# One load stream for the expert weights, and the float64 conversion spread over all experts, in a fused scan, mixture-of-experts and feed-forward kernel

## The chip, the cores and the metric

The kernel runs on one core of a Trainium2 chip. The metric is the time of one execution on the device in microseconds (us); 1192.2 us is the median of three runs before the change. The engines are named as the profile names them: PE is the matrix engine (PEld its weight loads), DVE the vector engine, ACT the scalar engine, POOL the GpSimd engine, and SP the engine that issues most of the DMA transfers. Each engine works through its own instructions strictly in order.

## The reference, cut to what matters

Three stages follow each other. The first is a recurrent scan over 768 positions for 32 (batch, head) pairs; the change does not touch it. Its output, 3072 rows of 320 values, goes through eight experts, one per row, and then through a dense pair of layers whose weights are given as float64:

```python
    logits = x @ w_gate
    e_idx = np.argmax(logits, axis=1)
    ...
    gate_w = probs[np.arange(N), e_idx]
    eom = 1.0 / (1.0 + np.exp(-(x @ w_output_gate)))
    for e in range(E):
        mask = e_idx == e
        h = np.maximum(x[mask] @ w1[e], 0.0)
        ye = h @ w2[e]
        out[mask] = gate_w[mask, None] * eom[mask, e, None] * ye
...
    h = np.maximum(x @ w_in, 0.0)
    return (h * h @ w_out).astype(np.float32)
```

## The kernel before, in words

The scan fills the first 560 us. It leaves the rows sorted by expert in a DRAM tile `xsD`, with the logits of each row beside it. Then come the experts, one after the other, and then the dense pair. All of it is written with a hand schedule: instructions stand on each engine in the order in which the Python code emits them.

**Weights in two parts.** Each weight is split into a high and a low float32r part. A piece of up to 732 columns is loaded from DRAM into one of four `raws` buffers (L909, on SP), ACT copies it rounded to the high part (L922), and POOL subtracts to get the low part (L923). An expert has eight such pieces. They go to one of two `ring` buffers, so the next expert's weights are split while this expert runs.

**An expert on PE.** The first layer has eight steps f of eight matmuls each (L1185, writing a PSUM tile `ph`, of which there are three). After each step ACT takes the high part of the hidden values (L1253) and DVE the low part (L1254); only then is that `ph` free again. In the last three steps PE also transposes the next expert's rows (L1226), which ACT and DVE split (L1175 to L1179). The second layer is 64 matmuls (L1356). Pieces of the next expert's weights are taken in steps f below 6 and early in the second layer.

**Gate factors.** `gates` computes, from the logits in `xg`, the token number and the squared factor of each row, in ten short instructions (eight on DVE: L987 to L999). It is emitted step by step within the first layer, between the L1254 instructions. The result `gt` goes to the DRAM tile `gtD` in two writes, one right behind the other (L1342).

**The float64 weights.** `widths` turns pairs of 32-bit words into float32. One step is: load `q` (L1141), one ACT instruction (L1151), four DVE instructions (L1152 to L1155), one POOL add (L1156), one more DVE instruction (L1167). Sixteen steps convert the first matrix `wi` beside the second layers of the experts, mostly three per expert, and the result goes to DRAM (`wiD`) and comes back as pieces. Sixteen steps of 320 columns convert `wo`, beside the last expert and the first steps of the dense pair; `split_o` splits each result at once (L1199 on ACT, L1200 on POOL).

**The dense pair.** 96 steps of `stage1` (eight matmuls L1185; then ACT L1404, DVE L1405, ACT L1407, DVE L1408) and, two steps behind, `stage2` (twelve matmuls L1188 to L1190). Before the first step the factors are read back into `GT` (L1383) and DVE copies the token numbers (L1384).

Of the kernel before, what the change touches and what calls it, by code (L numbers as in the profile page):

```python
# [7 lines left out]
F32 = mybir.dt.float32  # L8
# [23 lines left out]
NP = 104  # partitions of the (head of pair at 0 / 64, feature) layout  # L32
# [38 lines left out]
def layout(r, k, v, w, a, b, moe_w_gate, moe_w_output_gate, moe_w1, moe_w2, moe2_w_in, moe2_w_out):  # L71
# [41 lines left out]
ORDER = [  # stage, chunk relative to the iteration, argument  # L113
# [38 lines left out]
TAIL = [  # the last two iterations: stage, chunk relative to the last one, argument  # L152
# [73 lines left out]
HEAD = [  # the stages before the first regular iteration: stage, chunk, argument  # L226
# [70 lines left out]
EARLY = [2, 3, 5, 0]  # the first chunks for which DVE does a share of GpSimd's work  # L297


def attention(ctx, tc, nc, A, K, R, nch=NCH, order=ORDER, head=HEAD, tail=TAIL):  # L300
# [20 lines left out]
    def early(shape):  # L321
        """part of the arena: the buffers here are done with some chunks before the end"""
# [74 lines left out]
    # ---- loads  # L397
# [33 lines left out]
    # ---- decays: W (before a token) and C (after it), scaled a, b, k  # L431
# [20 lines left out]
    def A_rec2(c):  # L452
        # third-order step: 1 / C = y (t^2 - 3 t + 3), t = C y
# [27 lines left out]
    # ---- a.b and a.k of all pairs of tokens of a chunk  # L481
# [56 lines left out]
    # ---- inverse of the unit triangular system: 16 x 16 blocks, then the pair  # L538
# [65 lines left out]
    # ---- state  # L604
# [82 lines left out]
    # ---- outputs  # L687
# [72 lines left out]
    # ---- routing  # L760
# [49 lines left out]
def program(tc, A, out, nch=NCH, order=ORDER):  # L810
    nc = tc.nc
    V, G, S_, P = nc.vector, nc.gpsimd, nc.scalar, nc.tensor
    with ExitStack() as top:
# [6 lines left out]
        wiD = dp.tile([128, 3 * F2], F32, name="wiD")  # L820
        cst = cp.tile([128, C_TRI], F32, name="cst")
# [23 lines left out]
        # ---- routing of 128 tokens  # L845
# [28 lines left out]
        def beyond():  # L874
            """whether there are rows beyond CAP, or decays out of range, or too few of the rows that are read ahead"""
# [22 lines left out]
        W1E = [732 * i for i in range(7)] + [5120, 5632]  # pieces of an expert's weights, the last 64 columns of the second ones apart  # L898
        W2I = [768 * i for i in range(9)]

        def pieces(slot, src, at, slots=4):
            """weights as the sum of two float32r parts, piece by piece"""
# [11 lines left out]
            for i in range(len(at) - 1):  # L914
                rw = ahead.pop(i)
                if at[i + 1] == 5632:  # high and low parts side by side
                    rw = rw.rearrange("p (f x)->p f x", x=64)
                    both = ring[slot][:, 5120:6144].bitcast(F32R).rearrange("p (f x)->p f x", x=128)
                    hi, lo = both[:, :, 0:64], both[:, :, 64:128]
                else:  # L920
# [551 lines left out]
```

## Time and profile before

| | |
|---|---|
| median of three runs | 1192.2 us (1192.02 to 1195.96) |
| span of the profiled execution | 1201.3 us |
| instructions in the profile | 31764 |
| PE busy | 1038.2 us, 86% of the span |
| DVE busy | 829.3 us, 69% |
| ACT busy | 652.6 us, 54% |
| POOL busy | 476.9 us, 40% |
| DMA, mean over the span | 96 GB/s |

No time of the profiled execution is recorded besides its span, which is 0.8% above the median of the other runs. Busy shares are averages over three stages with different limits, so the reader should look at stages: the scan ends at about 560 us, the first matmul of the experts stands at 560.5 us, and the dense pair begins at 830.4 us. PE is busy for 86% of the span, but its busy time also counts matmuls that ran at the lower of its two clock levels.

### The profile page before, as it was taken

What the parts mean: (1) busy time and instruction counts of PE and PEld (TensorE: products, weight loads), DVE (VectorE), ACT (ScalarE), POOL (GpSimd) and SP (SyncE); (2) the same over time, 40 slices, a digit from 0 to 9 for tenths busy, and PEclk for the clock granted to TensorE, in tenths of its full rate; (3) what the DMA queues carried; (4) which work ended last, traced back from release to release, by engine and by line L of the source; (5) the groups of instructions that cost most, each with busy time, mean ns of one, the idle gap of its engine ahead of it and who ended that gap; (6) DMA issues with size and microseconds to landing.
All of it is one profiled execution on the core that took longest, in us unless ns stands there. A gap on an engine that the chain in (4) does not pass through costs nothing.

```text
span 1201.3 us, 31764 instructions
## 1 busy us (share of the span) xinstructions
PE 1038.2 (86%) x13114; PEld 911.5 (76%) x13114; DVE 829.3 (69%) x1827; ACT 652.6 (54%) x1407; POOL 476.9 (40%) x465
## 2 busy tenths in 40 slices
PE   2688888888897778887988889998989999999997
PEld 2577777777786666767877778886879998998986
DVE  6999998989989999653675566536993434344442
ACT  6587786776686776672444434334443343443432
POOL 6556464554554645341455455435541010101011
PEclk9977785869576886787989899999999999999999
DMA  5843333333332332243576667535330000000000
GB/s 139 265 124 83 87 93 86 98 83 92 86 92 72 104 86 70 82 122 125 133 200 168 179 188 187 146 115 131 104 97 23 27 23 27 23 1 23 2 21 22
DMA packets 56236, 114.99 MB, mean 96 GB/s; under 512 B 14608, under 2 KB 30096, under 8 KB 54160
## 3 DMA queue, kind: packets, MB, share of 16 engines
q1 hardware_dynamic: 50656, 100.47, 30.9%
q0 software_dynamic: 2688, 8.88, 1.9%
q10 hardware_dynamic: 2736, 3.49, 0.9%
q8 instruction: 106, 1.74, 0.6%
q14 instruction: 50, 0.41, 0.1%
HBM read 89.39 MB, written 23.43 MB: 94 GB/s over the span
## 4 chain that ended last, share of the span: by engine, by line
PE 31%; DVE 12%; DMA 6%; ACT 2%; issue 1%; SPq 1%; POOL 0%; POOLq 0%; ACTq 0%; DVEq 0%
PE ph L1185 17%; PE po L1189 4%; PE po L1190 4%; PE po L1188 4%; DMA raws<-in_we_dram 2%; PE py L1356 2%; DMA q<-in_wi_dram 2%; DVE c L1153 1%; DVE hl L1408 1%; DVE q L1405 1%; DVE c L1167 1%; DVE gm L996 1%; DVE gt L997 1%; DVE gt L999 1%; DVE c L1154 1%
## 5 line engine op out<-in xcount | busy, mean ns | idle before, releaser
L1185 PE MATMUL ph<-x,ring 128*128 128x512 f32 (+2 forms) x1344 | 319.7, 387 | 27.2 <-DVE hw L1254 27.2
L1185 PEld LDWEIGHTS ph<-x,ring 128*128 128x128 f32 x1344 | 249.5, 197 | 63.0 <-DVE hw L1254 30.0
L923 POOL TENSOR_TENSOR ring<-raws,ring 128x732 fp32r<-128x732 f32 (+2 forms) x72 | 124.1, 1744 | 137.2 <-ACT ring L922 108.3
L1405 DVE TENSOR_TENSOR q<-r 128x512 f32<-128x512 f32 x96 | 73.0, 761 | 106.8 <-ACT r L1404 106.8
L1423 POOL DMA_INDIRECT out_dram<-o,TID x24 | 28.2, 1175 | 269.6 <-ACT o L1421 226.7
L1189 PE MATMUL po<-ring,hl 128*128 128x320 f32 x368 | 115.6, 314 | 7.3 <-DVE hl L1408 7.3
L1188 PE MATMUL po<-ring,hh 128*128 128x320 f32 x368 | 114.6, 311 | 2.8 <-ACT hh L1407 2.8
L474 POOL TENSOR_TENSOR arena<-arena 40x1024 f32<-40x1024 f32 x43 | 108.5, 2523 | 20.2 <-ACT arena L456 16.0
L1404 ACT ACTIVATE r<-ph 128x512 f32<-128x512 f32 x96 | 57.1, 595 | 108.6 <-PE ph L1185 108.6
L1190 PE MATMUL po<-ring,hh 128*128 128x320 f32 x368 | 114.2, 310 | 0.0
L1408 DVE TENSOR_TENSOR hl<-q,hh 128x512 fp32r<-128x512 f32 x92 | 72.5, 788 | 54.8 <-ACT hh L1407 54.8
L1407 ACT ACTIVATE hh<-q 128x512 fp32r<-128x512 f32 x92 | 58.2, 633 | 88.0 <-DVE q L1405 88.0
L1356 PE MATMUL py<-hw,ring 128*128 128x448 f32 x512 | 105.4, 365 | 0.0
L1356 PEld LDWEIGHTS py<-hw,ring 128*128 128x128 f32 x512 | 95.5, 188 | 7.6
L1254 DVE SCALAR_TENSOR_TENSOR hw<-ph,hw 128x448 fp32r<-128x448 f32 (+2 forms) x72 | 39.7, 567 | 88.2 <-ACT hw L1253 88.1
L1189 PEld LDWEIGHTS po<-ring,hl 128*128 128x128 f32 x368 | 69.6, 189 | 14.9 <-DVE hl L1408 11.1
L1188 PEld LDWEIGHTS po<-ring,hh 128*128 128x128 f32 x368 | 69.8, 190 | 7.5 <-ACT hh L1407 3.2
L450 POOL TENSOR_TENSOR arena<-Cx,arena 104x512 f32<-104x512 f32 x22 | 26.3, 1197 | 123.6 <-ACT xs L862 115.7
L1190 PEld LDWEIGHTS po<-ring,hh 128*128 128x128 f32 x368 | 69.7, 189 | 0.0
L922 ACT ACTIVATE ring<-raws 128x732 fp32r<-128x732 f32 (+2 forms) x72 | 56.9, 792 | 22.8 <-DMA raws<-in_we_dram 20.5
L1253 ACT ACTIVATE hw<-ph 128x448 fp32r<-128x448 f32 (+2 forms) x72 | 35.8, 498 | 57.8 <-PE ph L1185 57.6
L439 DVE TENSOR_TENSOR_SCAN Cx<-arena 104x528 f32<-104x528 f32 x24 | 61.0, 2540 | 7.0 <-DMA arena<-in_xE_dram 6.3
(215 smaller groups left out, 2257.7 us busy)
## 6 DMA issues: line engine op xcount, KB each, us to landing
raws<-in_we_dram SPq DMA_DIRECT2D x48, 366.0 KB
arena<-in_xE_dram SPq DMA_DIRECT2D x48, 322.5 KB
xL<-in_xL_dram SPq DMA_DIRECT2D x24, 480.0 KB
xsD<-raws SPq DMA_DIRECT2D x24, 268.0 KB
q<-in_wi_dram SPq DMA_DIRECT2D x16, 384.0 KB
xg<-xsD SPq DMA_DIRECT2D x7, 804.0 KB
q<-in_wo_dram SPq DMA_DIRECT2D x16, 320.0 KB
wb<-in_wB_dram SPq DMA_DIRECT2D x24, 165.0 KB
```

The source lines that it names most:

```text
L439: V.tensor_tensor_scan(out=Cx.rearrange("p a b->p (a b)"), data0=s["w"], data1=d1[0:NP].rearrange("p a b->p (a b)"), initial=0.0, op0=ALU. ...
L474: (V if c < EARLY[2 + hh] else G).tensor_tensor(out=bd[sl, :, :, hh].rearrange("p a b c x->p (a b) c x"), in0=s["bk"][sl].rearrange("p (a ...
L923: G.tensor_tensor(out=lo, in0=rw, in1=hi.bitcast(F32), op=ALU.subtract)
L1185: P.matmul(ps, t[:, o : o + 128], x3[:, i, c], start=(j == 0), stop=(j == 7))
L1188: P.matmul(ps, hh, whi[:, o : o + 320], start=start, stop=False)
L1189: P.matmul(ps, hl, whi[:, o : o + 320], start=False, stop=False)
L1190: P.matmul(ps, hh, wlo[:, o : o + 320], start=False, stop=stop)
L1356: P.matmul(py, w, x, start=(f == 0 and k == 0), stop=last)
L1404: S_.activation(r, ph, AF.Relu)
L1405: V.tensor_tensor(out=q, in0=r, in1=r, op=ALU.mult)
L1407: S_.activation(hh, q, AF.Copy)
L1408: V.tensor_tensor(out=hl, in0=q, in1=hh.bitcast(F32), op=ALU.subtract)
```

## The change

All expert weights from expert 1 on, and then the converted `wi`, become one stream of 64 pieces through the four `raws` buffers: a load is issued as soon as the piece four places earlier has been split, across the border between experts. Four pieces are split in steps f = 0 to 3 of each first layer and four in the second layer, at every sixteenth matmul. A class `Narrow` converts all 32 slices of `wi` and `wo`, four per expert, at the odd places of the second layer; `wo` now goes through a DRAM tile of its own (`woD`) and is split in the dense pair in eight pieces of 640 columns, on ACT and DVE. The gate work moves from the first layer to the second, reads the logits from a copy (`gl`, made by ACT), and its tiles lie in the pool `mp`. The two writes of the factors no longer follow each other: the second is issued in the next expert's last first-layer step. `GT` is read back at step 4 of the dense pair and the token numbers are copied at step 9.

```diff
+        def stream(jobs, before, slots=4):
+            todo = [(n, slot, src, at, i) for n, (slot, src, at) in enumerate(jobs) for i in range(len(at) - 1)]
...
+            for j in range(slots):
+                load(j)
+            yield
+            for j, (_, slot, _, at, i) in enumerate(todo):
+                split(slot, at, i, ahead.pop(j))
+                load(j + slots)
+                yield
...
+            def step(self):
+                i = self.at
+                self.at += 1
+                if 0 <= i - 2 < len(self.todo):
+                    _, o, n, to = self.todo[i - 2]
+                    nc.scalar.dma_start(out=to[:, o : o + n], in_=self.c.pop(i - 2))
+                if i < len(self.todo):
+                    self.front(i)
...
+        def outer():
...
+            for i in range(8):
+                rw = ahead.pop(i)
+                hi, lo = (t[:, 640 * i : 640 * i + 640] for t in parts(ring[1], 5120))
+                S_.activation(hi, rw, AF.Copy)
+                V.tensor_tensor(out=lo, in0=rw, in1=hi.bitcast(F32), op=ALU.subtract)
+                load(i + 4)
+                yield
...
+                def factors(e, off):
+                    gt = mp.tile([128, 4, 2], F32, name="gt", bufs=2)
+                    yield from gates(mp, glog.pop(e), gt, e)
+                    yield
+                    put(0, 384, off, gt)
+                    rest.append((3, 64, off, gt))
...
-                        if f < 6 and (e or f % 2):
-                            drain(nxt[2], 1)
-                        drain(gate, 1)
+                        if f in (range(4) if e else (1, 3)):
+                            drain(later, 1)
+                        if e and 4 <= f < 7:
+                            narrow.load()
+                        if f == 7 and rest:
+                            put(*rest.pop())
...
+                def beside(e, t, gate):
+                    if t == 0 and e + 2 < E:
+                        load_x(e + 2)
+                    if t % 2 == 0:
+                        drain(later, 1)
+                    else:
+                        narrow.step()
+                    if t == 2:
+                        narrow.load()
+                    if t > 0:
+                        drain(gate, 1)
...
-                        if i % 16 == 0:
-                            beside(e, i // 16, nxt)
+                        if i % 8 == 0:
+                            beside(e, i // 8, gate)
...
-                    split_o(n + 1)
...
+                    if n % 2 == 0:
+                        drain(wout, 1)
+                    if n == 2:
+                        put(*rest.pop())
+                    if n == 4:
+                        nc.sync.dma_start(out=GT, in_=gtD[Y0 : Y0 + S * B].rearrange("(c p) x->p c x", p=128))
+                    if n == 9:
+                        V.tensor_copy(TID, GT[:, :, 0])
```

On DVE, in the first layer of a middle expert before the change (hw is the hidden low part, gm, gd and gt are the gate's tiles, pk the transposed rows):

```order
L1254 SCALAR_TENSOR_TENSOR hw<-ph,hw 128x448
L987 TENSOR_REDUCE gm<-xg 128x4
L988 TENSOR_TENSOR gd<-xg,gm 128x32
L1254 SCALAR_TENSOR_TENSOR hw<-ph,hw 128x448 x2
L993 COPY gt<-xg 128x4
L995 TENSOR_REDUCE gm<-gd 128x4
L996 TENSOR_SCALAR gm<-gm 128x4
L997 SCALAR_TENSOR_TENSOR gt<-gt,gm 128x4
L998 RECIPROCAL gt<-gt 128x4
L999 TENSOR_TENSOR gt<-gt 128x4
L1254 SCALAR_TENSOR_TENSOR hw<-ph,hw 128x448 x3
```

The same engine there after the change, from the first layer (L1294 is the former L1254) into the second:

```order
L1294 SCALAR_TENSOR_TENSOR hw<-ph,hw 128x448 x6
L1206 TENSOR_TENSOR x_13203<-pk,x_13203 128x448
...
L1200 SCALAR_TENSOR_TENSOR c_13081<-q_12998,c_13081 128x384
L1012 TENSOR_REDUCE gm<-gl 128x4
L1013 TENSOR_TENSOR gd<-gl,gm 128x32
L1405 TENSOR_TENSOR yT<-py,yT 64x448
...
L1018 COPY gt<-gl 128x4
L1020 TENSOR_REDUCE gm<-gd 128x4
L1021 TENSOR_SCALAR gm<-gm 128x4
L1022 SCALAR_TENSOR_TENSOR gt<-gt,gm 128x4
L1023 RECIPROCAL gt<-gt 128x4
L1024 TENSOR_TENSOR gt<-gt 128x4
```

The gate's eight DVE instructions have left the first layer and stand between the conversion steps of the second. On SP, from the end of an expert's second layer to the start of the next one's, before the change (yTD are the stores of an expert's result, raws the weight loads, xg the next rows):

```order
L909 DMA raws<-in_we_dram 128x732 x4
L1365 ISA
L1365 DMA yTD<-yT 128x448
L1322 TENSOR_LOAD oi
L1322 ISA x2
L909 DMA raws<-in_we_dram 128x732 x2
L909 DMA raws<-in_we_dram 128x728
L909 DMA raws<-in_we_dram 128x512
L1342 ISA
L1342 DMA gtD<-gt 128x3x2
L1342 ISA
L1342 DMA gtD<-gt 64x2
```

The same queue after the change, from one second layer's last store to the next second layer's first load (q are the float64 words):

```order
L1406 DMA yTD<-yT 128x448
L1363 TENSOR_LOAD oi
L1363 ISA x2
L947 DMA raws<-in_we_dram 128x732 x2
L947 DMA raws<-in_we_dram 128x728
L947 DMA raws<-in_we_dram 128x512
L1174 DMA q_12892<-in_wi_dram 128x768
L1174 DMA q_12905<-in_wi_dram 128x768
L1174 DMA q_12926<-in_wi_dram 128x768
L1333 ISA
L1333 DMA gtD<-gt 64x2
L1277 DMA xg<-xsD 128x4x402
```

Before, the loads of an expert's first four pieces stood behind everything that the previous second layer issued; now the loads stand four pieces ahead, and three loads of float64 words stand between them and the second write of the factors.

## Rows read from the trace of the kernel before

**Rows 1.** Stretches: length, busy us (instructions) of five engines, PE clock, DMA share, GB/s.

```profile
583.60:619.54 35.94, 31.44 (x142) 27.72 (x141) 20.72 (x34) 14.99 (x28) 18.60 (x12) 0.91 0.65 181
...
758.08:789.71 31.63, 29.66 (x142) 26.52 (x141) 17.82 (x26) 13.52 (x26) 14.77 (x9) 0.95 0.50 149
789.71:817.63 27.92, 26.21 (x129) 24.05 (x129) 11.44 (x19) 12.86 (x24) 13.17 (x8) 1.00 0.52 162
...
830.43:896.57 66.14, 56.08 (x278) 47.01 (x277) 59.45 (x102) 29.80 (x62) 32.20 (x29) 0.95 0.39 108
896.57:1201.30 304.73, 296.52 (x1644) 267.70 (x1643) 121.66 (x177) 117.61 (x202) 29.35 (x25) 0.99 0.05 19
600.00:606.00 6.00, 4.07 (x21) 3.48 (x20) 1.95 (x6) 2.72 (x7) 2.97 (x3) 1.00 1.01 391
```

**Rows 2.** Timeline of PE: start, us, instructions, idle before and its releaser.

```profile
578.77 1.89 PE L1185 MATMUL ph<-x,ring 128*128 128x256 f32 x8 [2.68 <-DVE hw L1254]
...
653.70 13.30 PE L1356 MATMUL py<-hw,ring 128*128 128x448 f32 x64
666.85 6.57 PE L1185 MATMUL ph<-x,ring 128*128 128x448 f32 x32
...
677.15 0.69 PE L1226 MATMUL pk<-cst,xg 128*128 128x128 f32 x4
682.02 3.36 PE L1185 MATMUL ph<-x,ring 128*128 128x448 f32 x8 [4.18 <-DVE hw L1254]
...
686.25 2.79 PE L1185 MATMUL ph<-x,ring 128*128 128x448 f32 x8
```

**Rows 3.** The chain that ended last, pieces in order of time: start, us, what.

```profile
582.89 9.41 DMA q<-in_wi_dram
...
666.19 5.66 DMA raws<-in_we_dram
...
681.44 0.54 DVE hw L1254
```

**Rows 4.** Timeline of DVE in the first layer of an expert.

```profile
676.25 0.17 DVE L995 TENSOR_REDUCE gm<-gd 128x4 f32<-128x32 f32 x1
676.45 1.59 DVE L996 TENSOR_SCALAR gm<-gm 128x4 f32<-128x4 f32 x1
678.08 1.65 DVE L997 SCALAR_TENSOR_TENSOR gt<-gt,gm 128x4 f32<-128x4 f32 x1
...
679.97 1.47 DVE L999 TENSOR_TENSOR gt<-gt 128x4 f32<-128x4 f32 x1
```

**Rows 5.** Timeline of POOL, first layer and the second layer behind it.

```profile
672.81 10.30 POOL L923 TENSOR_TENSOR ring<-raws,ring 128x732 fp32r<-128x732 f32 x6 [6.84 <-ACT ring L922]
690.99 1.97 POOL L923 TENSOR_TENSOR ring<-raws,ring 128x728 fp32r<-128x728 f32 x1 [7.87 <-ACT ring L922]
694.10 1.20 POOL L1156 TENSOR_TENSOR c<-c,r 128x384 int32<-128x384 int32 x1 [1.15 <-ACT ring L922]
```

**Rows 6.** Timeline of DVE in that second layer, which PE begins at 689.50.

```profile
690.97 0.36 DVE L1152 TENSOR_SCALAR c<-q 128x384 int32<-128x384 int32 x1
...
694.46 0.62 DVE L1364 TENSOR_TENSOR yT<-py,yT 64x448 f32<-64x448 f32 x1
...
698.75 0.48 DVE L1152 TENSOR_SCALAR c<-q 128x384 int32<-128x384 int32 x1 [0.60 <-DMA q<-in_wi_dram]
...
700.34 0.55 DVE L1167 SCALAR_TENSOR_TENSOR c<-q,c 128x384 int32<-128x384 int32 x1
```

**Rows 7.** Timeline of PE in the first steps of the dense pair.

```profile
838.99 0.63 PE L1188 MATMUL po<-ring,hh 128*128 128x320 f32 x1 [2.81 <-ACT hh L1407]
...
896.41 2.02 PE L1185 MATMUL ph<-x,ring 128*128 128x512 f32 x8
900.02 2.02 PE L1185 MATMUL ph<-x,ring 128*128 128x512 f32 x8
```

**Rows 8.** Who waited for whom from 583 to 830 us: us, times, longest.

```profile
ACT ring L922 <- DMA raws<-in_we_dram: 20.0, 15, 3.8
```

More of the change, by code (lines that the diff above doesn't have):

```diff
@@ L914, in pieces @@
             for i in range(len(at) - 1):
[L915 to L920, printed above, removed]
-                    hi, lo = (t[:, at[i] : at[i + 1]] for t in parts(ring[slot], 6144))
-                S_.activation(hi, rw, AF.Copy)
-                G.tensor_tensor(out=lo, in0=rw, in1=hi.bitcast(F32), op=ALU.subtract)
+                split(slot, at, i, ahead.pop(i))
                 load(i + slots)
@@ L930, in drain, with load @@
                     return
+        def stream(jobs, before, slots=4):
+            todo = [(n, slot, src, at, i) for n, (slot, src, at) in enumerate(jobs) for i in range(len(at) - 1)]
+            ahead = {}
+            def load(j):
+                if j < len(todo):
+                    n, _, src, at, i = todo[j]
+                    if i == 0:
+                        before(n)
+                    ahead[j] = raws[:, nld[0] % slots, 0 : at[i + 1] - at[i]]
+                    nld[0] += 1
+                    nc.sync.dma_start(out=ahead[j], in_=src[:, at[i] : at[i + 1]])
+            for j in range(slots):
[5 more added lines that the diff above has]
+                yield
         first_w = []
@@ L992, in gates @@
             yield
[L993 removed]
+            V.tensor_copy(g[..., 0], x[..., 16])
             g = g[..., 1]
@@ L1131, in program, with __init__, load, front @@
         xg, x3 = {}, {}
[L1133 to L1148 removed]
+        class Narrow:
+            def __init__(self):
+                self.todo = [(A["wi"].bitcast(I32), o, 384, wiD) for o in range(0, 3 * F2, 384)]
+                self.first = len(self.todo)
+                self.todo += [(A["wo"].bitcast(I32), o, 320, woD) for o in range(0, 5120, 320)]
+                self.at, self.loaded, self.q, self.c = 0, 0, {}, {}
+            def load(self):
+                i = self.loaded
+                self.loaded += 1
+                if i < len(self.todo):
+                    src, o, n, _ = self.todo[i]
+                    self.q[i] = mp.tile([128, 384, 2], I32, name="q64", bufs=4)[:, 0:n]
+                    nc.sync.dma_start(out=self.q[i].rearrange("p n w->p (n w)"), in_=src[:, 2 * o : 2 * (o + n)])
+            def front(self, i):
+                q, n = self.q[i], self.todo[i][2]
+                c, r = mp.tile([128, 384], F32, name="c64", bufs=4)[:, 0:n], mp.tile([128, 384], I32, name="r64", bufs=2)[:, 0:n]
                 ci = c.bitcast(I32)
[L1150 removed]
+                self.c[i] = c
                 S_.activation(r, q[:, :, 0].bitcast(U32), AF.Copy, scale=2.0**-29)
@@ L1256, in hidden, with before @@
                 )
-            def next_w(e):
-                w = (*parts(ring[e % 2], 6144), pieces(e % 2, *((A["we"][e], W1E) if e < E else (wiD, W2I))))
-                drain(w[2], 1)
-                return w
-            def work():
-                ready = {}
-                def store():
-                    for o in list(ready):
-                        nc.scalar.dma_start(out=wiD[:, o : o + 384], in_=ready.pop(o))
-                for _ in widths(A["wi"], 3 * F2, 384, ready):
-                    yield
-                    store()
-                store()
+            def before(n):
+                assert n + 1 < E or narrow.at > narrow.first + 1
             with tc.manual_schedule():
@@ L1284, in program @@
                 cur = parts(ring[0], 6144)
-                later = next_w(1)
+                narrow = Narrow()
+                later = stream([(e % 2, A["we"][e], W1E) for e in range(1, E)] + [(0, wiD, W2I)], before)
+                drain(later, 1)
                 load_x(1)
@@ L1313, in program, with put @@
-                wide = work()
-                wout = widths(A["wo"], 5120, 320, cast)
+                        drain(later, 1)
+                    if f < 4:
+                        narrow.load()
+                    if f == 7:
+                        narrow.step()
+                def put(j, n, off, gt):
+                    why = "the experts have at most S * B rows together"
+                    p = min(n, 128)
+                    at = nc.s_assert_within(off + 128 * j, 0, YR - n, skip_runtime_bounds_check_because=why)
+                    nc.sync.dma_start(out=gtD[bass.ds(at, n)].rearrange("(j p) x->p j x", p=p), in_=gt[0:p, j : j + n // p])
```

106 lines of the change are left out of this document (39 added, 67 removed).

## The prediction

> **What bounds the kernel now.** I read the stretches first, one per expert, from the start of one second layer to the start of the next [rows 1]. From 583.60 to 789.71 stand six of them, 206.1 us together; the first takes 35.94, the last 31.63. The seventh, in which nothing is transposed, takes 27.92. No engine fills a stretch: in the first, PE is busy for 31.4 of 35.9 us, DVE for 20.7, POOL for 18.6. So there are waits, and the PE timeline shows where [rows 2]. The 64 matmuls of a second layer take 13.30 us with their tail, 13.1 from start to start. Half a first layer takes 6.57, so a whole one 13.1. Three groups of transposes add 0.63 each, 1.9. An expert without waits is thus 28.1 us, the seventh 26.2. Against that the first six stretches hold 206.1 - 168.6 = 37.5 us too much and the seventh 1.7: **39.2 us** of excess.
>
> Its form is always the same. At 682.02 PE has waited 4.18 us for DVE's L1254, and then runs slowly: eight matmuls take 3.36 and 2.79 us where a quarter of 6.57 is 1.64 [rows 2]. The granted clock of the first stretch is 0.91 and of the sixth 0.95, but 1.00 in the seventh, where PE hardly waits [rows 1]: right behind its idle time PE ran at the lower of its two levels, 1.2 GHz, where a matmul takes twice as long. What held L1254? The DVE timeline answers [rows 4]: in front of it stand the gate instructions, three of which take 1.47 to 1.65 us for four elements, while a reduction of the same size takes 0.17. POOL runs six splits back to back then, 10.30 us, 1.72 each, so with ends at 676.24, 677.96, 679.68 and 681.39 [rows 5]; each slow instruction ends within 0.1 us behind one of these ends, so each waited for a POOL instruction. And POOL's six stand in a row because ACT had waited for their loads: the chain has a load that began at 666.19 and took 5.66 us, and then L1254 at 681.44 [rows 3]. In all ACT waited 20.0 us for such loads [rows 8].
>
> The dense pair has a second loss. Its steps follow each other every 3.61 us once the wo slices are done [rows 7]. Two groups of stage1, 2.02 each, and 13 steps would bring the start of step 15 from 830.43 to 881.4; it stands at 896.41, **15.0 us** late. In that stretch DVE is busy for 59.45 of 66.14 us [rows 1].
>
> **The change, part by part.** *Gates out of the first layer.* From 676.25 to 681.44 DVE does nothing else but gates, 5.2 us; PE's wait of 4.18 and most of the slow matmuls behind it go. *Loads ahead.* With a lead of four pieces the load is issued when POOL has split the piece four places earlier, and four pieces are half an expert's, some 14 us; POOL may lag ACT by 5 of them, and in the 9 that are left the 5.66 us of the chain [rows 3] fit, so I cost these waits at nothing. If the cover is gone, 20.0 us stay. *More bytes.* By the sizes in the code each expert now moves 2.9 MB of weights, four slices of 0.39 and their four stores of half that, 0.8 of rows and 0.6 of results: 6.6 MB in 28.1 us, 236 GB/s. From 600 to 606 the queues moved 391 GB/s at a share of 1.01 [rows 1], so this is some 60% of what they did.
>
> *Where the stall goes.* What is late next is DVE in the second layer. It begins there 1.5 us behind PE (690.97 against 689.50) and a conversion step takes 3.5 us with a split beside it (690.97 to 694.46), 2.1 without (698.75 to 700.89) [rows 6]. Now there are four steps, each with a split beside it: I take 3.3 each, 13.2. One yT sum adds 0.55. The eight gate instructions add 1.5 if none is held (0.17 to 0.2 each) and 5.2 or more if held as in [rows 4]; POOL has only two instructions to run into there, so I take 2.7. The sum is 16.5, and DVE comes free 18.0 us behind the start of the second layer. Its first L1254 then ends at 18.6. PE starts the next first layer at 13.1 and fills its three `ph` in 4.9, so from 18.0 on it waits, 0.6 us. I take **1.0 us per expert**, to leave some for the three loads of float64 words that now stand right ahead of the second layer, and no loss of clock for so short a wait. Seven times 1.0 leaves 32.2 of the 39.2 us. From below: with free steps (2.1 each) and free gates DVE is done at 1.5 + 10.5 = 12.0, PE never waits, and all 39.2 us come back. From above: steps of 3.5 and gates of 6.8 (5.2 and a held copy) end at 22.8, PE waits 5.4 us and loses another 2.9 at the lower clock (3.36 + 2.79 - 2 x 1.64), 8.3 per expert, 58 in all: 19 us worse than now. I take a value near the lower end because POOL, with pieces of 1.97 and adds of 1.20 spread over the second layer [rows 5], is not busy back to back as it was in the gate rows.
>
> On just this the Trainium skill, "SBUF — State Buffer", section "SBUF: two separate sides", has a rule: DVE in a two-port mode or with two SBUF inputs and a POOL instruction exclude each other, and the one that started first keeps the ports for its whole length. The trace agrees in the gate rows, where the held ones end with POOL's and the reduction is free. The rule speaks against this change, as it puts all four steps and the gates beside POOL's work; by it the holds are at most POOL's own work there, four splits and four adds, which brings the sum to the second rival's end and not past it.
>
> *First expert.* The same gates hold PE for 2.68 us at 578.77, and the eight matmuls behind take 1.89 instead of half of that [rows 2]: 3.5 us come back; from below 0, if the four slice loads that are new there delay ACT as much.
>
> *ACT and POOL.* ACT gets one copy of 72 columns per expert and one more conversion; it is busy for 15 of 36 us [rows 1], and its wait for PE hides this. POOL's eight splits and four adds come to 18.5 us of 28.1. The wo split that POOL did moves to DVE in the dense pair, one instruction of 640 columns in every second step; behind 896.57 DVE is busy for 121.66 of 304.73 us [rows 1], 1.4 of each 3.61, so there is room.
>
> *Factor writes.* Two writes in a row hold SP while the first lands; they are apart now. SP's loads are ahead anyway, so I give this nothing of its own: at most it is part of the 20.0 us.
>
> *The dense pair.* The steps at 3.61 return the 15.0 us less a slow start. woD's first load can only go out behind the last store of results, which ACT delays by a conversion step (estimate: 2.5 us after the pair begins), and takes up to 5.7 us [rows 3]; ACT and DVE then split, so stage2 starts near 8 us instead of 5.6, and PE, having stood idle, runs slowly for a while, as it did behind 838.99, where it had waited 2.81 [rows 7]. I leave 5.0 us and take 10.3; bounds 6 and 14.
>
> **The sum.** 3.5 + 32.2 + 10.3 = 46.0 us. The profiled execution goes from 1201.3 to 1155.3, and the median, 0.8% below its span, from 1192.2 to about **1147 us**.
>
> **Rivals.** *(a) DVE becomes the bound of the second layer.* Many of the 28 instructions that POOL can hold there are held. For it: L1153 and the gates were held wherever POOL ran. Against it: POOL has work for 11 of 13 us there and cannot hold longer. Midway PE loses 4.2 us per expert: 39.2 - 29 + 13.8 (the first expert and the dense pair) = 24 us gained, about 1168. At the end of the scale 19 lost against 13.8 gained: 1197, no change. *(b) The loads are no earlier.* A load waits for POOL to free its buffer, and POOL's order is set by ACT and DVE. If ACT keeps its 20.0 us of waits, 39.2 - 20.0 + 13.8 = 33 us are gained: 1160. So the change would not do the half of what it says. *(c) Slower.* The instruction order shows that every transfer waits for the one eight places before it. An expert has 22 of them now. If each takes L us to land, a stretch cannot be shorter than 22 x L / 8: 15.6 us at 5.66, 25.9 at the 9.41 of the slowest load I saw [rows 3]. It decides from L = 10.2; at 14 a stretch takes 38.5, 4.1 more than now on average, and 25 us lost in six against 13.8 gained give 1203.
>
> **How the numbers follow.** The forecast gets 0.62, (a) 0.22, (b) 0.12, (c) 0.04. The forecast's own range is 1135 (all excess gone: 3.5 + 39.2 + 14 = 57 us) to 1160 (two more us per expert). The range that is to hold 8 in 10 reaches to (b) and to the middle of (a): 1135 to 1175. Beyond it lie the far half of (a) and (c). A measurement here tells 0.5% (6 us) from no change. Faster by more: all of the forecast and (b) and most of (a), 0.89. Within: the end of (a), 0.05. Slower: (c) and the worst of (a), 0.06.
>
> **What the profile of the changed kernel will show.** If I am right: stretches of about 29 us from one second layer to the next, a clock of 0.97 or more in them, PE's waits for the hidden low part below 1.5 us and now ahead of the fourth step instead of the seventh, no gate instruction between them, ACT's waits for weight loads below 5 us in all, and dense steps of 3.61 from the fourth on. Waits of 3 us and more ahead of the fourth step, with DVE still in its conversion steps, speak for (a); ACT idle for loads in the first layer for (b); SP waiting on transfers that land late for (c). The forecast would be most wrong through DVE's 16.5 us: each us more there is a us per expert, and more with the clock.

## The result, and the profile after the change

The changed kernel takes **1155.6 us** (median of four runs, 1148.13 to 1160.31) against 1193.1 us (1192.02 to 1195.96) beside it: a ratio of 0.9698, 95% interval [0.9639, 0.9758]. Two repeats gave 0.9689 and 0.9718 (below). Medians here are over all executions, while ratios leave out three in a slower state (two of the kernel before, one of "all pieces in the first layer").

Medians hide where the time went, so every profiled execution is cut at three marks on the PE timeline: the first matmul of the first expert, the start of the first second layer, the first matmul of the dense pair. What lies ahead is the scan, which the change leaves alone. All numbers in us; the names are those of the experiments. The stages come from one profiled execution each, the median from all executions of the kernel.

| kernel | first expert | experts | dense pair | from first matmul to end | median |
|---|---|---|---|---|---|
| before | 23.1 | 246.8 | 370.9 | 640.8 | 1193.1 |
| before, second profile | 23.4 | 239.3 | 369.9 | 632.6 | 1189.7 |
| changed | 21.1 | 213.0 | 362.9 | 597.0 | 1155.6 |
| changed, two repeats | 20.9, 20.7 | 213.5, 213.3 | 362.3, 362.6 | 596.6, 596.6 | 1156.0, 1156.9 |
| gates only | 19.2 | 263.6 | 374.0 | 656.7 | 1209.8 |
| gates, writes parted | 19.1 | 236.7 | 373.7 | 629.5 | 1187.6 |
| gates back | 21.8 | 227.3 | 358.4 | 607.5 | 1164.1 |
| lead of two | 20.7 | 238.6 | 360.6 | 619.8 | 1178.6 |
| writes together | 20.9 | 214.6 | 364.7 | 600.3 | 1156.0 |
| all pieces in the first layer | 21.1 | 215.0 | 357.1 | 593.2 | 1150.9 |
| late stores | 20.3 | 213.7 | 359.1 | 593.1 | 1155.0 |
| step early | 21.7 | 209.7 | 359.7 | 591.1 | 1149.1 |
| six and two | 20.6 | 217.2 | 357.2 | 595.0 | 1151.4 |

First the stretches of the changed kernel, from one second layer to the next and then two of the dense pair, with the columns of [rows 1]:

```profile
570.37:599.55 29.18, 28.79 (x142) 25.24 (x141) 22.26 (x40) 15.19 (x29) 18.42 (x12) 1.00 0.66 186
...
628.97:658.47 29.50, 28.78 (x142) 25.24 (x141) 21.98 (x40) 15.29 (x30) 18.29 (x12) 1.00 0.84 228
...
716.03:744.21 28.18, 28.18 (x142) 25.35 (x141) 21.51 (x40) 15.34 (x30) 17.64 (x12) 1.00 0.86 227
744.21:770.27 26.06, 26.06 (x130) 24.07 (x129) 19.80 (x37) 13.95 (x28) 17.98 (x12) 1.00 0.68 182
783.41:849.55 66.14, 62.09 (x327) 54.82 (x326) 37.30 (x56) 28.63 (x48) 4.37 (x3) 0.97 0.37 81
```

A stretch is 28.2 to 29.5 us instead of 31.6 to 35.9, at a granted clock of 1.00: the matmuls of the experts no longer run at the lower level. The PE timeline of the third stretch answers to [rows 2]:

```profile
628.97 13.48 PE L1397 MATMUL py<-hw,ring 128*128 128x448 f32 x64
642.29 5.09 PE L1215 MATMUL ph<-x,ring 128*128 128x448 f32 x24
648.09 5.19 PE L1215 MATMUL ph<-x,ring 128*128 128x448 f32 x24 [0.72 <-DVE hw L1294]
653.12 0.69 PE L1266 MATMUL pk<-cst,xg 128*128 128x128 f32 x4
```

The wait of 4.18 us ahead of the seventh step is gone; one of 0.72 stands ahead of the fourth. The DVE timeline of that second layer answers to [rows 4, 6]:

```profile
631.26 1.18 DVE L1183 TENSOR_SCALAR c<-q 128x384 int32<-128x384 int32 x1 [0.85 <-DMA q<-in_wi_dram]
...
634.22 0.79 DVE L1013 TENSOR_TENSOR gd<-gl,gm 128x32 f32<-128x32 f32 x1
...
638.48 0.98 DVE L1018 COPY gt<-gl 128x4 f32<-128x4 f32 x1
639.38 0.17 DVE L1020 TENSOR_REDUCE gm<-gd 128x4 f32<-128x32 f32 x1
639.58 1.59 DVE L1021 TENSOR_SCALAR gm<-gm 128x4 f32<-128x4 f32 x1
...
644.91 1.33 DVE L1184 TENSOR_SCALAR c<-c 128x384 f32<-128x384 f32 x1
...
647.42 1.68 DVE L1294 SCALAR_TENSOR_TENSOR hw<-ph,hw 128x448 fp32r<-128x448 f32 x3
```

Here one DVE instruction is long for each POOL instruction that it meets (L1183 1.18, L1021 1.59, L1184 1.33; the same lines take 0.36, 0.17 and 0.36 elsewhere), and then, while POOL is idle, several run free. DVE comes to L1294 at 647.42, 18.4 us behind PE's start. Whole waits from 570 to 783 us, who for whom (us in total, times, longest), answer to [rows 8]:

```profile
PE ph L1215 <- DVE hw L1294: 2.9, 4, 1.0
```

```profile
ACT ring L909 <- DMA raws<-in_we_dram: 0.6, 2, 0.3
```

The dense pair begins less smoothly than forecast. ACT there, then PE, which answers to [rows 7]:

```profile
787.88 0.54 ACT L1402 ACTIVATE yT<-py 128x448 f32<-128x448 f32 x1 [3.69 <-DVE c L1200]
790.33 0.33 ACTq L1195 DMA_DIRECT2D woD<-c  x1
790.70 0.60 ACT L1443 ACTIVATE r<-ph 128x512 f32<-128x512 f32 x1 [2.28 <-DVE c L1200]
```

```profile
791.35 3.69 PE L1215 MATMUL ph<-x,ring 128*128 128x512 f32 x8 [4.05 <-ACT r L1443]
796.64 2.03 PE L1215 MATMUL ph<-x,ring 128*128 128x512 f32 x8
```

ACT stands at the store of the last converted slices (L1195, on its queue) until DVE has made them (L1200), and so takes the first group's result (L1443) only at 790.70. PE waits 4.05 us, and eight matmuls then take 3.69 us instead of 2.03, the lower level. From 796.64 on the steps follow each other every 3.63 us.

### The profile page after: what moved, and what is told of

Read it like the earlier page. It is cut to its first block, busy times and chain, and to the rows that moved or that the text cites. A ratio compares the mean times of both kernels' runs of the same rounds, so it can differ in the third digit from the quotient of the medians.

```text
span 1146.3 us, 31807 instructions
## 1 busy us (share of the span) xinstructions
PE 1017.2 (89%) x13114; PEld 894.1 (78%) x13114; DVE 814.8 (71%) x1835; ACT 654.8 (57%) x1407; POOL 462.0 (40%) x449
## 4 chain that ended last, share of the span: by engine, by line
PE 39%; DVE 8%; DMA 3%; issue 1%; ACT 0%; POOL 0%; SPq 0%; POOLq 0%; ACTq 0%; DVEq 0%
PE ph L1215 22%; PE po L1219 5%; PE po L1218 5%; PE po L1220 5%; PE py L1397 2%; DVE c L1183 2%; DVE c L1184 1%; DMA q<-in_wi_dram 1%; DVE c L1200 1%; DVE gm L1021 1%; PE pk L1266 1%; DVE c L1185 1%; DMA out_dram<-o,TID 1%; DMA q<-in_wo_dram 1%; DVE c L1186 1%
## 5 line engine op out<-in xcount | busy, mean ns | idle before, releaser
L1215 PE MATMUL ph<-x,ring 128*128 128x512 f32 (+2 forms) x1344 | 310.8, 379 | 8.2 <-DVE hw L1294 4.2
L1215 PEld LDWEIGHTS ph<-x,ring 128*128 128x128 f32 x1344 | 240.8, 190 | 45.0 <-DVE hw L1294 6.2
L1469 POOL DMA_INDIRECT out_dram<-o,TID x24 | 28.2, 1176 | 323.3 <-ACT o L1467 280.5
L1444 DVE TENSOR_TENSOR q<-r 128x512 f32<-128x512 f32 x96 | 66.5, 692 | 121.9 <-ACT r L1443 121.9
L910 POOL TENSOR_TENSOR ring<-raws,ring 128x732 fp32r<-128x732 f32 (+2 forms) x72 | 124.2, 1741 | 67.2 <-DVE x L1209 28.2
L1443 ACT ACTIVATE r<-ph 128x512 f32<-128x512 f32 x96 | 57.5, 599 | 126.3 <-PE ph L1215 124.1
L474 POOL TENSOR_TENSOR arena<-arena 40x1024 f32<-40x1024 f32 x43 | 111.6, 2595 | 26.1 <-ACT arena L456 15.9
L1446 DVE TENSOR_TENSOR hl<-q,hh 128x512 fp32r<-128x512 f32 x92 | 63.7, 693 | 64.2 <-ACT hh L1445 64.2
L1294 DVE SCALAR_TENSOR_TENSOR hw<-ph,hw 128x448 fp32r<-128x448 f32 (+2 forms) x72 | 40.0, 570 | 48.4 <-ACT hw L1293 48.3
L684 PE MATMUL tp<-cst,sT 104*80 104x104 f32 x368 | 56.7, 297 | 0.0
```

The costliest lines, as they stand in the source:

```text
L474: (V if c < EARLY[2 + hh] else G).tensor_tensor(out=bd[sl, :, :, hh].rearrange("p a b c x->p (a b) c x"), in0=s["bk"][sl].rearrange("p (a ...
L910: G.tensor_tensor(out=lo, in0=rw, in1=hi.bitcast(F32), op=ALU.subtract)
L1215: P.matmul(ps, t[:, o : o + 128], x3[:, i, c], start=(j == 0), stop=(j == 7))
L1443: S_.activation(r, ph, AF.Relu)
L1444: V.tensor_tensor(out=q, in0=r, in1=r, op=ALU.mult)
L1446: V.tensor_tensor(out=hl, in0=q, in1=hh.bitcast(F32), op=ALU.subtract)
```

## The experiments

**The change as a whole, again, beside the next three.**

> The changed kernel unaltered, a second profile of it. My theory (the change works only from the first expert on, and the scan's own time differs from execution to execution): the stretch from the first expert's second layer to the dense pair is again 213 us within 1 and the dense pair 363 within 1, while the start of the experts, 549.3 in the first profile of it and 560.5 in that of before, moves by several us. Rival (the change makes the scan shorter too, for example by where its tiles lie): the experts start within 2 us of 549.3 again.

Measured: 1156.0 us, ratio 0.9689 [0.9645, 0.9733]; experts 213.5, dense pair 362.3. The experts began at 560.0 us, not within 2 us of 549.3: so the early start in the first profile was not a gain of the change, and the rival falls.

**The gates alone** moved into the second layer, on the kernel before. Both factor writes go along:

```diff
+                        if i % 8 == 0 and i:
+                            drain(gate, 1)
+                        if i == 32:
+                            for j, n in ((0, 384), (3, 64)):
...
-                        drain(gate, 1)
```

> The kernel before with one part of the change: the gate work is moved to the second layer and reads a copy of the logits; the loads and the conversion stay as they were. My theory (the held gates stand in front of the hidden low part and stop PE; the late loads cost by making POOL run in a row): PE's waits of about 4 us ahead of the seventh step vanish, the experts take 247 - 20 to 247 - 28, that is 219 to 227 us; what is left is ACT's 20 us of waits for weight loads, partly covered by three ph. Rival 1 (the late loads alone are the cause, through ACT): 240 us or more, since ACT waits for its loads as before. Rival 2 (the gates alone): 213 to 217 us, the whole gain.

Measured: 1209.8 us, ratio 1.0149 [1.0115, 1.0184], 1.5% **slower**. The theory is wrong. The experts' 263.6 us lie in rival 1's "240 us or more", but ACT did not wait "as before": its load waits rose from 20.0 to 51.9 us, and no theory had expected a loss. SP, ACT and PE of one expert, whose second layer PE began at 655.70, with SP's waits for these writes in all the experts (us, times, longest) ahead of them:

```profile
SPq L1353 <- DMA gtD<-gt: 25.4, 7, 4.8
```

```profile
669.03 4.54 SPq L1353 DMA_DIRECT2D gtD<-gt  x2
673.82 0.38 SPq L1369 DMA_DIRECT2D yTD<-yT  x1
674.31 1.82 SPq L909 DMA_DIRECT2D raws<-in_we_dram  x4
```

```profile
680.24 0.81 ACT L922 ACTIVATE ring<-raws 128x732 fp32r<-128x732 f32 x1 [9.05 <-DMA raws<-in_we_dram]
```

```profile
682.19 5.90 PE L1185 MATMUL ph<-x,ring 128*128 128x448 f32 x16 [6.79 <-DVE hw L1254]
```

The second write waits for the first, so the pair holds SP for 4.5 us (it did so in the kernel before too, but there behind the loads), and the next weights are queued behind it: issued 18.6 us behind the start of the second layer, 12.5 in the kernel before [rows 2, 3]. Everything behind them in ACT's order waits, PE for 6.79 us. Whether the writes do it shows when the second write is put off.

**Gates alone, writes parted.**

```diff
-                            for j, n in ((0, 384), (3, 64)):
...
+                            put(0, 384, off, gt)
+                            if e < E - 1:
+                                rest.append((3, 64, off, gt))
...
+                        if f == 7 and rest:
+                            put(*rest.pop())
```

> The kernel before with the gates alone moved into the second layer, as in the run of the gates alone, but with the second factor write put off to the next expert's last first-layer step. Theory (that run was slower because SP stood between the two writes ahead of the next expert's loads, which went out 18.6 us behind the start of the second layer, 12.5 in the kernel before): the loads go out 4 to 6 us earlier, ACT's waits for raws loads fall from 51.9 us to 20 to 30, experts 232 to 247 us instead of 263.6, median at or below the kernel before, up to 10 us. Rival (the late loads come from DVE's gates and conversion steps themselves, on which the first write and the results wait): loads no earlier, ACT's waits over 45 us, experts over 257.

Measured: 1187.6 us, ratio 1.0010 [0.9985, 1.0035]; experts 236.7 us; ACT's load waits 33.5, a little above the theory's figure. In an expert whose second layer began at 642.35:

```profile
657.00 1.82 SPq L909 DMA_DIRECT2D raws<-in_we_dram  x4
```

```profile
664.20 0.81 ACT L922 ACTIVATE ring<-raws 128x732 fp32r<-128x732 f32 x1 [6.36 <-DMA raws<-in_we_dram]
```

```profile
666.15 5.05 PE L1185 MATMUL ph<-x,ring 128*128 128x448 f32 x16 [4.09 <-DVE hw L1254]
```

The loads go out 14.7 us behind it, 3.9 earlier, and the experts take 27 us less than in the run before: parting the writes carries that, and the rival falls. By the ratios it is worth less, 1.4% or some 17 us; the profiled execution of "gates only" took 1217.5 us, its median is 1209.8. But there is still no gain over the kernel before. PE waits 4.09 us, now ahead of the fifth step. The releaser named is DVE, yet DVE had been idle; it waited for ACT, and ACT for the load. So the gates and the late loads had held PE *one behind the other's cover*: without the gates, the loads alone cost about as much. Part of that cost is new, though: the loads still go out 2.2 us later than in the kernel before, and ACT waits 33.5 us for them instead of 20.0. What the loads at their old time would cost without the gates is not shown.

**Gates back** in the first layer, all else as changed (the second write then follows the first again):

```diff
-                    if t > 0:
-                        drain(gate, 1)
...
+                        drain(gate, 1)
```

> The changed kernel with the gate work back between the hidden low parts of the first layer; stream, even split, conversion and writes as changed. My theory: POOL's four splits in the first layer hold the gates there again, PE waits 1 to 3 us in the middle of the first layer, but DVE is free about 4 us earlier in the second layer, so that the wait ahead of the fourth step goes; experts 215 to 228 us. Rival 1 (loads alone): 213 us or less, the place of the gates does not matter once POOL's splits are spread. Rival 2 (gates alone): 235 us or more, most of the gain lost.

Measured: 1164.1 us, ratio 0.9783 [0.9751, 0.9814]; experts 227.3, 14 us above the changed kernel, near the upper end of the theory. DVE in a first layer and PE behind it:

```profile
660.12 1.60 DVE L1021 TENSOR_SCALAR gm<-gm 128x4 f32<-128x4 f32 x1
661.76 1.67 DVE L1022 SCALAR_TENSOR_TENSOR gt<-gt,gm 128x4 f32<-128x4 f32 x1
```

```profile
665.71 1.91 PE L1215 MATMUL ph<-x,ring 128*128 128x448 f32 x8 [2.01 <-DVE hw L1294]
```

The old rows return with loads that are on time: ACT has no wait for weights in this run. Against the second profile of before (239.3) the change with the gates left in gives 12.0 us of experts, the gates alone 2.6 (writes parted), both together 26. Against the first (246.8) it is 19.5, 10.1 and 33.8. Either way the two do not add up to the whole. The median of the gates alone, no different from before, fits the second profile, where the time from the first matmul to the end falls by 632.6 - 629.5 = 3.1 us, and not the first, with 11.3.

**A lead of two pieces** instead of four:

```diff
-        def stream(jobs, before, slots=4):
+        def stream(jobs, before, slots=2):
```

> The changed kernel with a lead of two pieces instead of four (two of the four buffers stay unused). My theory: a load now goes out 3.5 us ahead of its use in the first layer and takes up to 5.7 to land, so ACT waits about 2 us per piece in the first layer, 6 to 8 per expert, of which three ph cover some 4; experts 225 to 240 us. Rival (the lead does not matter, only that the order is even and the gates are gone): 213 to 216 us.

Measured: 1178.6 us, ratio 0.9890 [0.9849, 0.9931]; experts 238.6, as the theory had it. ACT's waits and PE's longest:

```profile
ACT ring L909 <- DMA raws<-in_we_dram: 62.9, 30, 4.4
```

```profile
799.04 5.02 PE L1215 MATMUL ph<-x,ring 128*128 128x448 f32 x16 [5.26 <-DVE hw L1294]
```

The lead itself is worth 25 us of experts. Without it, all but one us of the change's gain there over the second profile of before is gone.

**Repeat for the next three.**

> The changed kernel once more, for comparison with the three that run beside it. Experts, from the first second layer to the first matmul of the dense pair, 213 to 214 us; dense pair from there to the end of the span 362 to 363; median within 0.5% of 1156 us.

Measured: 1156.9 us, ratio 0.9718 [0.9673, 0.9762]; experts 213.3, dense pair 362.6, as expected.

**Both writes together**, as before, in the changed kernel (`put(3, 64, off, gt)` right behind the first):

> The changed kernel, with the two factor writes again one right behind the other, in the second layer. Theory (the lead of four pieces covers what SP loses while the first write lands, 3.5 to 4.5 us per expert): experts 213 us plus or minus 1.5, median within 0.3% of the changed kernel. Rival (parting the writes is worth something of its own, because loads land late behind them, as when the gates alone were moved): ACT waits for raws loads over 10 us in all, experts over 218 us, median 5 us or more above.

Measured: 1156.0 us, ratio 0.9711 [0.9670, 0.9752], no difference; experts 214.6. ACT's waits and PE's show why:

```profile
ACT ring L909 <- DMA raws<-in_we_dram: 17.4, 6, 3.3
```

```profile
PE ph L1215 <- DVE hw L1294: 3.2, 5, 1.0
```

ACT does wait for loads, as the rival said, but it had that time to spare, and PE's waits are those of the changed kernel (2.9). With the lead, parting the writes is worth 1.3 us of experts at most; without it, it was worth 27 between two profiles and some 17 by the ratios. The dense pair is 2.1 us longer than in the repeat; why is not shown, and the medians do not show it.

**All eight pieces in the first layer.**

```diff
-                    if t % 2 == 0:
-                        drain(later, 1)
-                    else:
+                    if t % 2:
...
-                        if f in (range(4) if e else (1, 3)):
+                        if f in (range(8) if e else (1, 2, 3, 4, 5, 6)):
```

> The changed kernel, with all eight pieces of an expert split in the eight steps of the first layer and none in the second layer. Theory (what is left of PE's waits for the hidden low part comes from POOL's splits holding DVE's conversion in the second layer): those waits, 2.9 us in the changed kernel, fall below 0.5, and the excess of the experts from 5.3 to about 2, experts about 210, unless ACT now waits for loads. Rival (the even split is itself what keeps the loads ahead; eight pieces in 13 us ask the queues for 330 GB/s while the second layer leaves them idle for pieces): ACT waits for raws loads over 10 us, L1294 comes late in the first layer, experts 217 to 235 us.

Measured: 1150.9 us, ratio 0.9628 [0.9571, 0.9684]; experts 215.0, dense pair 357.1. Neither theory fits: PE still waits 4.7 us for the low part, and ACT 9.6 for weights. Without splits beside it no DVE instruction of a conversion step is held; a step takes 1.93 us (644.92 to 646.85), where the changed kernel's four take 1.94 to 3.72, 11.3 in all. But ACT now waits for the float64 words:

```profile
ACT r L1182 <- DMA q<-in_wo_dram: 22.0, 9, 6.2
ACT r L1182 <- DMA q<-in_wi_dram: 18.7, 5, 6.8
```

```profile
649.07 9.07 DMA q<-in_wi_dram
```

```profile
658.24 0.36 DVE L1183 TENSOR_SCALAR c<-q 128x384 int32<-128x384 int32 x1 [4.01 <-DMA q<-in_wi_dram]
```

The fourth step's words are on their way for 9.07 us, among the next weights: from 645 to 650 us the queues move 362 GB/s at a share of 1.02. What the free steps give, these late words take. What this run gains stands in the dense pair (357.1 against 362.6), whose fourth group of stage1 starts 7.4 us behind the pair's start; why it starts so early was not tried.

**Late stores:** the last two conversion steps in dense steps 1 and 3.

```diff
-                    else:
+                    elif e < E - 1 or t < 7:
                         narrow.step()
...
+                    if n in (1, 3):
+                        narrow.step()
```

> The changed kernel, with the last two conversion steps moved from the end of the last second layer into the dense pair, at its steps 1 and 3. Theory (the start of the dense pair is held by ACT, which stands at the store of the last converted slice until DVE has made it): the wait of 4.05 us ahead of the third group of stage1 goes, the half-clock matmuls behind it too, dense pair 357 to 359 us instead of 362 to 363, median 3 to 6 us below the changed kernel. Rival (the slow start comes from woD's first load, as the prediction had it): the load is now later still, the wait moves to stage2, dense pair 362 us or more.

Measured: 1155.0 us, ratio 0.9699 [0.9656, 0.9741]; dense pair 359.1, 3.5 less; by the median 1.9 less, which the interval does not tell from no change. PE:

```profile
787.10 5.78 PE L1215 MATMUL ph<-x,ring 128*128 128x512 f32 x24
793.33 0.41 PE L1218 MATMUL po<-ring,hh 128*128 128x320 f32 x1 [0.45 <-ACT ring L1238]
...
796.60 2.02 PE L1215 MATMUL ph<-x,ring 128*128 128x512 f32 x8
```

The wait of 4.05 us is gone as the theory had it, though less comes of it than the 3 to 6 us by the median. Three groups run through, and the fourth starts 9.5 us behind the pair's start instead of 13.2. ACT's store had held it. What is left is a wait of 0.45 us for the split of the first wo piece (L1238), which ACT takes behind its other work, and two short ones for DVE. The load of that piece, the prediction's own term, does not show: in the changed kernel SP issues it 8.3 us ahead of the pair's start, and ACT never waits for a wo piece there or here.

```profile
775.15 0.34 SPq L1230 DMA_DIRECT2D raws<-woD  x1
```

**Step early:** as late stores, and each second layer's fourth conversion step moved to step 5 of the next first layer.

```diff
+                        if e and f == 5:
+                            narrow.step()
```

> The changed kernel with the last two conversion steps in the dense pair, and from expert 1 on the last conversion step of each second layer moved to step 5 of the first layer. Theory (the waits ahead of the fourth step come from DVE's chain of four conversion steps and the gates, 18.4 us long where PE has 18.0): the chain is some 3 us shorter, no wait of PE for the hidden low part in middle experts, experts 207 to 210 us instead of 213 to 214, dense pair 357 to 359 as with the late steps alone, median 6 to 10 us below the changed kernel, 1146 to 1150. Rival (DVE's conversion step within the first layer delays L1294 there as the gates did before): a wait ahead of step 7 or ahead of the next second layer, experts 214 us or more.

Measured: 1149.1 us, ratio 0.9643 [0.9611, 0.9676]; experts 209.7, as expected; dense pair 359.7, a little above. The experts as one stretch:

```profile
580.12:789.84 209.72, 209.72 (x1033) 188.11 (x1033) 154.56 (x298) 114.50 (x215) 133.05 (x89) 1.00 0.74 220
```

PE is busy in all of it at the high level. So the waits of the changed kernel were DVE's chain in the second layer. This is the shortest of the kernels from the first expert to the end (591.1 against 596.6 to 597.0); in medians 6.5 to 7.8 us below the changed kernel, but the intervals of the ratios overlap a little, and no changed kernel ran beside it.

**Six pieces and two,** otherwise as step early.

```diff
-                        if f in (range(4) if e else (1, 3)):
+                        if f in (range(6) if e else (1, 3, 4, 5)):
...
-                    if t % 2 == 0:
+                    if t in (0, 4):
```

> The kernel of the run before it, with six pieces of an expert split in the first layer and two in the second. Theory (POOL's splits hold DVE in the second layer, and the all-in-the-first-layer version failed to gain only because its float64 words came late): PE does not wait, experts 207 to 209 us, the same or up to 1.5 us less than with four and four. Rival (more splits in the first layer hold L1294 there, and loads come too close): ACT waits for raws loads over 10 us, PE waits for the hidden low part again, experts 211 to 216 us.

Measured: 1151.4 us, ratio 0.9688 [0.9663, 0.9714]; experts 217.2, outside both ranges; ACT's waits for raws loads are 2.7 us, not the rival's 10. Stretches one to six are those of step early (28.2 and 28.5), as the theory had it; the last expert loses 7.5 us:

```profile
769.66 0.84 ACT L909 ACTIVATE ring<-raws 128x768 fp32r<-128x768 f32 x1 [2.67 <-DMA raws<-wiD]
```

```profile
777.55 1.12 PE L1399 MATMUL py<-hw,ring 128*128 128x448 f32 x2 [3.55 <-DVE hw L1294]
```

There the fifth wi piece comes late, and the conversion step and the dense rows' splits then stand ahead of L1294 at once.

**The kernel before, profiled again.**

> The kernel before, profiled a second time, to see which stage makes the 8 to 9 us by which its first profiled execution lay above the median of its timed runs, while the changed kernel's lies below its own. Theory (the scan, whose instructions are the same in both kernels, takes another time in each execution, as between three executions of the changed kernel, whose experts begin at 549.3, 560.0 and 555.4 us): experts 247 us plus or minus 2 and dense pair 371 plus or minus 2 again, the difference in the start of the experts, 545 to 565 us. Rival (the kernel before has itself executions with shorter experts): experts 240 us or less.

Measured: 1189.7 us, ratio 0.9994 [0.9970, 1.0018]. Experts 239.3 us: the rival was right. The experts of the two executions, first profile first:

```profile
583.60:830.43 246.83, 222.29 (x1033) 198.37 (x1033) 147.00 (x233) 104.53 (x193) 122.48 (x78) 0.93 0.61 166
```

```profile
585.34:824.65 239.31, 215.33 (x1034) 192.96 (x1034) 145.51 (x234) 105.21 (x194) 123.21 (x78) 0.96 0.62 171
```

PE is busy for 7.0 us less with the same matmuls, at a clock of 0.96 instead of 0.93, though its waits for the hidden low part are nearly equal (24.0 against 24.5 us). Thus 7.0 of the 7.5 us are matmuls at the lower level.

## Why the prediction was right, and where its sizes were off

The forecast of 1147 us was 8.6 us low; its mechanism holds.

- **The stall goes where it was said to go.** DVE free 18.0 us behind the start of the second layer, PE's wait 0.6 us ahead of the fourth step: measured 18.4 and 0.72 in the expert shown; in all four waits, 0.4 to 1.0, and none in the three with 320-column slices. That the sum came so close is partly luck, as its parts were off and cancelled: start 2.3 instead of 1.5 (0.85 of it a wait for float64 words), four steps 11.3 instead of 13.2, gates 4.3 instead of 2.7. "Step early" shows that this chain is all that was left. Rival (a) does not hold.
- **The loads.** ACT's 20.0 us of load waits became 0.6. "Lead of two" and "gates back" show that both parts are needed; the prediction treated them as one sum and was saved by making both. That one hides the other was not in it: "gates alone" was expected to take 20 to 28 us off the experts, and even with the writes parted its median gains nothing. Rival (b) does not hold.
- **Excess of the experts.** This term failed in size. Its 39.2 us came from one execution; by the same reckoning (28.1 and 26.2) the second profile holds 31.7, and the changed kernel 5.1. Recovered are 34.1 or 26.6 us, where 32.2 were forecast. The prediction scaled its sum by the 0.8% by which the span lay above the median, as if that were spread over all; against the second profile it lay in the experts, where the matmuls behind a wait had run longer at the lower level. From the first matmul to the end the change takes 640.8 - 596.7 = 44.1 us off the profile that the sum was made on, near the 46.0 forecast; the timed runs gained 37.5. Stages can be seen in profiled executions only, so how long the experts took in the timed runs is not known; but from the second profile the sum is 632.6 - 596.7 = 35.9, and the medians differ by 35.2 to 37.5.
- **Dense pair.** 10.3 forecast (15.0 less 5.0 is in fact 10.0), 7.0 to 8.6 measured. Its late start was put down to woD's first load, which is out 8.3 us ahead of the pair. Three and a half us of it were ACT's store, which waits for DVE's last conversion and stands ahead of L1443 ("late stores"). The row to see was in ACT's own order. That the gain itself comes from the conversion and the split of wo being moved is read from the steps, 3.63 us each from the fourth group on; no run put them back.
- **First expert.** 3.5 forecast; 2.0 to 2.7 measured. The gates alone give 4.0 there (19.1 against 23.1); the rest of the change takes back 1.8. The trace has 1.26 of it, a wait of PE where a conversion step stands ahead of L1294 and one of its instructions takes 1.81 us beside a split of POOL, instead of 0.36:

```profile
560.95 1.81 DVE L1185 TENSOR_SCALAR c<-c 128x384 int32<-128x384 int32 x1
```

```profile
563.48 3.09 PE L1215 MATMUL ph<-x,ring 128*128 128x256 f32 x24 [1.26 <-DVE hw L1294]
```

- **Factor writes.** Nothing of their own: right with the lead, and only with it (1.3 us of experts; without the lead 27 between two profiles, some 17 by the ratios).
- **Eight in flight (c).** Stretches two to six of the changed kernel carry 222 to 228 GB/s at a share of 0.81 to 0.86, not the 60% of the estimate. Weights did not come late for it; the float64 words did, by 1.9 us in all for `wi` and 3.8 for `wo`, without a wait of PE beyond those above. Rival (c) does not hold.

The rule of the Trainium skill, "SBUF — State Buffer", section "SBUF: two separate sides", which the prediction tells, bears on the held instructions. The traces agree in kind: in the stretches read here, held ones appear only beside POOL's work. They set its size: in the changed kernel the four steps take 11.3 us beside POOL's splits and would take 7.7 at the free 1.93, so 3.6 us are lost on them, and 2.8 on the gates (4.3 instead of 1.5). That is 6.4 us of the 11.5 that POOL works there. The end that the prediction expects by the rule, the whole of POOL's work, is that of rival (a), the first of its list and not the second.

## What to carry to other kernels

When two causes hold one engine at nearly the same moment, taking one away can show little or even a loss, because the other was under its cover, or because the edit itself makes the other worse, as moving the gates made the loads later: list what would end the wait next before pricing an edit. A load that stands on an in-order queue behind a write that waits for the write before it is late by that write's landing, 4.5 us here; lead in the stream made such holds harmless, and parting them then brought nothing clear of noise. Before a sum is made against one profiled execution, compare its stages with a second one, above all where matmuls run at two levels.

## What was not expected of the hardware

The experts, behind the same instructions of the scan, began at 549 to 562 us in fourteen executions. The granted clock wanders between stretches of nearly the same work; the changed kernel and "all pieces in the first layer" from 300 to 400 us:

```profile
300.00:400.00 100.00, 86.59 (x1918) 75.69 (x1921) 94.00 (x245) 71.61 (x177) 54.48 (x56) 0.68 0.33 85
```

```profile
300.00:400.00 100.00, 76.27 (x1968) 64.59 (x1969) 97.52 (x243) 73.07 (x179) 54.18 (x63) 0.81 0.34 90
```

At 0.81 PE did more instructions in less busy time. Yet the execution with 0.81 came to its experts at 561.1 us and the one with 0.68 at 549.3, so the clock of one stretch does not tell the scan's length. And a wait does not always bring the lower level: in "gates back" eight matmuls took 1.91 us behind a wait of 2.01 (shown above), and 2.77 behind one of 1.84 in another expert:

```profile
602.82 2.77 PE L1215 MATMUL ph<-x,ring 128*128 128x448 f32 x8 [1.84 <-DVE hw L1294]
```

This fits with nearly equal waits and experts 7.5 us longer in one execution of the kernel before; what decides the level behind a wait is not shown.
